# A fixed order for the first job's preparation and the first four attention tiles, and word loads that wait for the first keys

## The chip, the cores and the metric

The program runs on one core of one Trainium2 chip. Its engines work side by side, each from its own queue, in order: TensorE (PE, with its weight loads as PEld), VectorE (DVE), ScalarE (ACT), GpSimd (POOL) and SyncE (SP), which here only issues DMAs. The metric is the device time of one execution in microseconds: 747.5 us for the kernel before, the median of three runs (747.46 to 748.02).

## What is computed

Three layers, one after the other: an attention over 2 batches of 8 heads with 576 rows of 64 columns, in which scores further than tau below their row's maximum are left out; a layer of three products, of which the largest counts, and a fourth product; and four experts, weighted by given shares.

```python
scores = scale * np.matmul(q, k.transpose(0, 1, 3, 2))
thresh = np.max(scores, axis=-1, keepdims=True) - tau
scores = np.where(scores >= thresh, scores, -1000000000.0)
attn = softmax(scores); attn_out = np.matmul(attn, v)
x = attn_out, as 1152 rows of 512
h = np.maximum(np.maximum(x @ w1, x @ w2), x @ w3)
x = h @ w_out
p = domain_probs / (domain_probs.sum(-1, keepdims=True) + 1e-09)
for e in range(4):
    h = np.maximum(x @ m_w1[e], 0.0)
    out += p[:, e:e + 1] * (h @ m_w2[e])
```

`w1`, `w2`, `w3` and `w_out` are 64-bit floats. The kernel loads them as pairs of 32-bit words and makes 32-bit floats of them itself.

## The kernel before

**Stages.** The work on batch 0 comes first. Its attention (stage A, `attention_fast`) has the chip to itself, apart from a little weight preparation. Then come the products on batch 0's rows, with batch 1's attention (`attention_slow`) woven in, and last the products on the rest. All products are matmuls issued at L832.

**Jobs and tiles.** A job is a pair of heads of one batch; stage A has four. A job's 576 rows are 512 main rows and a remainder of 64, and it is worked off in nine tiles: four row chunks for each of the two heads and one tile with both remainders. One tile passes through these steps: scores on PE (`qk`, L301), their negated maximum on DVE (`peak`, L312), the exponential on ACT (`power`, L319), the weighting on DVE, which drops what lies under the threshold and adds up the row (`weigh`, L324), the norm on POOL (`norm`, L332), transposes on PE (`turn`, L342, L345), and the cut of the transposed tile into a high and a low part (`cut_hi`, `cut_lo`; for some tiles through PE, for others through POOL). A group of tiles ends with the product with the values (`gather`, L418). In the code step i does tile i's maximum, the scores of tile i+1 and the cut of tile i-2.

**Preparation of a job.** Queries and keys are split into a high and a low part, transposed on PE and copied out of PSUM to the tiles `K` and `QS` (`prep`; for the first job `prep_first`, L198). Values are split by `values` (L240). The loads are `load_job` and, for the first job, `load_first`, both on SP but for the first queries, which ACT issues. `krem`, `qrem` and `vrem` are the remainders.

**Weight blocks.** A block of the 64-bit weights goes through: its load (`words`, L638), `exponent` on ACT (L646), `clamp` on POOL (L656), the shift `low3` (L653), `merge` (L659) and `sign` (L664) on DVE, `keep`, which writes the 32-bit block back to DRAM (L670), and `hi` and `lo` (L626, L630), which cut it for the matmuls. Each step is put on a list with a due time, counted in columns of products, by a table of lags; the first three blocks have a table of their own (`LAGS_FIRST`). `stream.flush(x)` issues all steps due until x. Up to three blocks (`EARLY`) put their `low3` tile into the PSUM pool of the transposes, and four blocks of words fit at a time (`NW`).

**What sets the order.** In the first attention stage nothing is fixed (`ORDER_A` is empty): the steps are written down in the order of the code, and a scheduler with a clock of its own puts every engine's queue in order. The later stages keep PE, DVE, ACT and POOL in the order of the code. On each engine, SP too, an instruction that waits holds up all that stand behind it. There are eight DMA semaphores, used in turn, so a DMA can't be issued until the eighth one before it has landed.

## Time and profile before

| | |
|---|---|
| Median of three runs | 747.5 us (747.46 to 748.02) |
| The profiled execution | 749.09 us, its span 747.3 us |
| Busy in the span | PE 96%, DVE 51%, ACT 45%, POOL 53% |
| First product matmul | 107.66 us after the start |
| Chain that ended last, share of PE | 77% |

The span is the time from the first to the last instruction of the profiled execution; all times in the rows below count from its start. A row of the timeline gives the start, how long it took, the engine, the line, the operation, the output and inputs, and in brackets how long the engine had been idle and what ended that. `SPq` is SP issuing a DMA, and the time is that of the issue, not of the transfer. In the rows `st_negm` is a tile's maximum, `em` its exponentials, `t` a tile of the transposes' PSUM pool, `a` a cut weight block and `b` the exponent part of one.

### The profile page before, as it was taken

The numbers are of one execution on the slowest core, as the hardware profiler recorded it, in microseconds if no ns is written. First come the engines' busy times: TensorE is split into PE (matmuls) and PEld (weight loads), VectorE is DVE, ScalarE is ACT, GpSimd is POOL, SyncE is SP. The second block draws the span as 40 slices with busy tenths as digits, with TensorE's granted clock in tenths as the row PEclk, the third lists the DMA queues.
The fourth block names the chain that finished last, engine by engine and source line by source line (L and its number), as shares of the span: only waits on it lengthen the run. The fifth ranks groups of instructions, "written<-read, shape, count | busy, mean of one in ns | idle before, by whom it ended". The sixth has DMA issues, their size and how long they took to land.

```text
span 747.3 us, 11716 instructions
## 1 busy us (share of the span) xinstructions
PE 715.7 (96%) x4103; PEld 636.4 (85%) x4103; DVE 378.3 (51%) x900; ACT 339.0 (45%) x716; POOL 392.4 (53%) x435
## 2 busy tenths in 40 slices
PE   4798999999899999999999999999999999999997
PEld 3787889777688788888888899999998998998996
DVE  6798988775265765766766421112222222222222
ACT  5688984444544655465454412333321321321320
POOL 5789785777554555564564524544623522522520
PEclk9799999999999999999999999999999999999999
DMA  6702006876724124122322233223412313312303
GB/s 183 227 22 49 1 1 187 261 226 204 199 78 113 59 73 122 57 73 57 86 61 66 71 113 85 68 58 91 132 50 85 99 43 85 104 45 77 113 2 71
DMA packets 89369, 71.01 MB, mean 95 GB/s; under 512 B 24158, under 2 KB 75358, under 8 KB 89310
## 3 DMA queue, kind: packets, MB, share of 16 engines
q1 hardware_dynamic: 88860, 69.96, 32.7%
q8 instruction: 33, 0.54, 0.3%
q10 hardware_dynamic: 418, 0.30, 0.2%
q14 instruction: 26, 0.21, 0.1%
q0 software_dynamic: 32, 0.00, 0.0%
HBM read 61.59 MB, written 8.65 MB: 94 GB/s over the span
## 4 chain that ended last, share of the span: by engine, by line
PE 77%; DVE 5%; ACT 5%; POOL 5%; issue 3%; DMA 3%; SPq 1%; POOLq 0%; ACTq 0%; DVEq 0%
PE ps L832 63%; PE u L418 5%; PE s L301 4%; PE t L342 3%; POOL a L630 2%; DVE st_negm L312 1%; DMA vrem<-in_v_dram 1%; ACT em L319 1%; DMA words<-in_moe_w_dram 1%; POOL b L656 1%; PE u L175 1%; DMA krem<-in_k_dram 1%; DVE raw L664 1%; ACT a L626 1%; PE t L388 1%
## 5 line engine op out<-in xcount | busy, mean ns | idle before, releaser
L630 POOL TENSOR_TENSOR a<-raw,a 128x512 fp32r<-128x512 f32 (+1 forms) x116 | 145.1, 1256 | 163.6 <-ACT a L626 160.3
L832 PE MATMUL ps<-b,hh 128*128 128x512 f32 x576 | 184.3, 393 | 0.0
L832 PEld LDWEIGHTS ps<-b,hh 128*128 128x128 f32 x576 | 107.3, 188 | 20.4
L782 ACT ACTIVATE hh<-ps 128x320 fp32r<-128x320 f32 (+1 forms) x96 | 46.8, 488 | 152.3 <-PE ps L832 151.9
L832 PE MATMUL ps<-b,hl 128*128 128x512 f32 x288 | 113.1, 393 | 0.0
L832 PE MATMUL ps<-y1h,a 128*128 128x320 f32 x512 | 112.8, 309 | 0.0
L630 POOL TENSOR_TENSOR b<-raw,b 128x512 fp32r<-128x512 f32 x64 | 82.8, 1296 | 53.4 <-ACT b L626 53.4
L785 DVE SCALAR_TENSOR_TENSOR hl<-ps,hh 128x320 fp32r<-128x320 f32 (+1 forms) x96 | 53.4, 556 | 108.9 <-ACT hh L782 108.8
L626 ACT ACTIVATE a<-raw 128x512 fp32r<-128x512 f32 (+1 forms) x116 | 69.4, 612 | 58.8 <-PE ps L832 19.1
L801 DVE SCALAR_TENSOR_TENSOR acc<-ps,pr,acc 128x512 f32<-128x512 f32 x63 | 47.2, 749 | 80.4 <-PE ps L832 80.3
L832 PE MATMUL ps<-y0h,a 128*128 128x512 f32 x256 | 85.1, 403 | 0.8 <-POOL a L630 0.8
L832 PEld LDWEIGHTS ps<-y1h,a 128*128 128x128 f32 x512 | 85.4, 188 | 0.3
L319 ACT ACTIVATE em<-s,st_negm 128x576 f32<-128x576 f32 x72 | 53.3, 744 | 70.9 <-DVE st_negm L312 70.7
L332 POOL TENSOR_SCALAR em<-em,st_r,even 128x576 f32<-128x576 f32 x70 | 57.5, 824 | 43.2 <-DVE st_r L331 41.6
L832 PE MATMUL ps<-y1l,a 128*128 128x320 f32 x256 | 79.1, 309 | 0.0
L312 DVE TENSOR_REDUCE st_negm<-s 128x1 f32<-128x576 f32 x72 | 54.1, 753 | 48.9 <-PE s L301 48.4
L301 PE MATMUL s<-K,QS 128*128 128x288 f32 x320 | 59.7, 315 | 6.4 <-DVE em L324 3.2
L832 PE MATMUL ps<-x1h,a 128*128 128x320 f32 x288 | 63.4, 309 | 0.0
L324 DVE SCALAR_TENSOR_TENSOR em<-s,st_thr,em 128x576 f32<-128x576 f32 x72 | 58.2, 812 | 9.9 <-ACT em L319 7.8
L832 PEld LDWEIGHTS ps<-b,hl 128*128 128x128 f32 x288 | 54.1, 188 | 10.0
L301 PEld LDWEIGHTS s<-K,QS 128*128 128x128 f32 x320 | 49.8, 197 | 11.3 <-issue 6.0
L832 PEld LDWEIGHTS ps<-y0h,a 128*128 128x128 f32 x256 | 47.8, 191 | 9.6 <-POOL a L630 1.2
(129 smaller groups left out, 1271.1 us busy)
## 6 DMA issues: line engine op xcount, KB each, us to landing
raw<-in_moe_w_dram SPq DMA_DIRECT2D x128, 256.0 KB
words<-in_moe_w_dram SPq DMA_DIRECT2D x18, 512.0 KB
kept_w<-raw SPq DMA_DIRECT2D x18, 256.0 KB
raw<-kept_w SPq DMA_DIRECT2D x18, 256.0 KB
kraw<-in_k_dram SPq DMA_DIRECT2D x30, 128.0 KB
words<-in_moe_w_out_dram SPq DMA_DIRECT2D x8, 384.0 KB
vraw<-in_v_dram SPq DMA_DIRECT2D x8, 256.0 KB
qraw<-in_q_dram SPq DMA_DIRECT2D x7, 256.0 KB
```

Source lines behind the costliest of these rows:

```text
L301: nc.tensor.matmul(st.s[:, kh, 0:HS], lhsT=l, rhs=r, start=i == 0, stop=i == len(terms) - 1)
L312: nc.vector.tensor_reduce(out=st.stat["negm"], in_=views(st)[0], op=ALU.max, axis=AX.XY, negate=True)
L319: nc.scalar.activation(out=ev, in_=sv, func=AF.Exp, bias=st.stat["negm"])
L324: nc.vector.scalar_tensor_tensor(out=ev, in0=sv, scalar=st.stat["thr"], in1=ev, op0=ALU.is_ge, op1=ALU.mult, accum_out=st.stat["sum"])
L332: last = (nc.vector if swift else nc.gpsimd).tensor_scalar(out=em, in0=em, scalar1=re, scalar2=even, op0=ALU.mult, op1=ALU.add)
L418: at["valued"] = nc.tensor.matmul(pv, lhsT=l, rhs=r, start=i == 0, stop=i == len(terms) - 1)
L626: nc.scalar.activation(out=b["hi"], in_=b["raw"], func=AF.Copy)
L630: nc.gpsimd.tensor_tensor(out=b["lo"], in0=b["raw"], in1=f32(b["hi"]), op=ALU.subtract)
L782: nc.scalar.activation(out=hs[f][0][:, a:z], in_=ps, func=AF.Relu)
L785: nc.vector.scalar_tensor_tensor(out=hs[f][1][:, a:z], in0=ps, scalar=0.0, in1=f32(hs[f][0][:, a:z]), op0=ALU.max, op1=ALU.subtract)
L801: nc.vector.scalar_tensor_tensor(out=accs[t], in0=ps, scalar=pe, in1=accs[t], op0=ALU.mult, op1=ALU.add)
L832: nc.tensor.matmul(ps, lhsT=l, rhs=r, start=i == 0, stop=i == count - 1)
```

## The change

`prep_first` is written anew: the same operations, in an order that puts the remainder's steps between those of the first head, and cut into pieces by `yield`. From its first piece to the end of the fourth tile's step all five engines, SP among them, keep the order of the code. The first three weight blocks lose their table: each load gets a due time in the head (`FIRST`), and its other steps a due time in one of three turns (`TURN`), which are flushed at set places in the steps of tiles 0, 1, 2 and 3. The constants for tau move behind the first scores, the first job's values into step 1, the second job's loads into the head, and the probabilities' loads behind the third job's. Before its first load of words, a one-column write to the words' tile from `krem` is put on DVE; the load has to wait for it, and it waits for the first keys' remainder.

```diff
-    READY = 20000
+    FIRST, TURN = -60000, -50000
-    LOAD_A, PREP_A, LOAD_B, PREP_B = 0, 1, 1, 3
+    LOAD_A, PREP_0, PREP_A, LOAD_B, PREP_B = 0, 3, 1, 1, 3
...
+        for h in range(2):
+            twin(h)
+            high(h)
+            low(h)
+            tk = turned(ks, h)
+            nc.scalar.activation(out=kd[h], in_=tk, func=AF.Copy)
+            tq = turned(qn, h)
+            if h == 0:
+                twin(2)
+                at["begun"] = kr[:, 1, 0:1]
+                yield
+                high(2)
+                tr = ptile_at("T", [P, 2, P])
+                trk, trq = (tr[:, i, :].rearrange("p (h r) -> p h r", h=2) for i in range(2))
+                nc.tensor.transpose(tr[:, 0, :], flat(kr), ident)
+            nc.scalar.activation(out=qd[h], in_=tq, func=AF.Copy, scale=SCALE)
+            if h:
+                yield
+            nc.vector.tensor_tensor(out=k2[h], in0=tk, in1=f32(kd[h]), op=ALU.subtract)
+            if h == 0:
+                nc.scalar.activation(out=k1r, in_=trk, func=AF.Copy)
+                nc.vector.tensor_tensor(out=k2r, in0=trk, in1=f32(k1r), op=ALU.subtract)
+                yield
+        low(2)
+        nc.tensor.transpose(tr[:, 1, :], flat(QN[:, 2 * NC]), ident)
...
         load_first(jobs[0])
-        stream.flush(-55000)
-        load_job(jobs[0], "v")
+        head = ExitStack()
+        head.enter_context(tc.manual_schedule(engines=set(names.values()) | {ENG.SP}))
         start = prep_first(jobs[0])
         next(start)
+
+        stream.flush(FIRST)
+        next(start)
         qk(steps[0])
+        constants()
+        load_job(jobs[0], "v")
+        stream.flush(FIRST + 1)
+        load_job(jobs[1], "qk")
+        stream.flush(FIRST + 2)
+        load_job(jobs[1], "v")
+        next(start)
+        peak(steps[0])
         for _ in start:
             pass
-        stream.flush(-READY)
-        back.add(values(jobs[0]))
...
+            if 0 < i <= EARLY:
+                stream.flush(TURN + 1000 * i - 1)
             if nxt:
                 power(st)
+            if i < EARLY:
+                stream.flush(TURN + 1000 * i + 100)
             if old:
                 cut_lo(old)
             if nxt:
                 limit(st)
+            if i < EARLY:
+                stream.flush(TURN + 1000 * i + 200)
+            if i == 1:
+                for _ in values(jobs[0]):
+                    pass
...
+            if i == EARLY:
+                head.close()
...
+            if "begun" in at and kept.setdefault("begun", True):
+
+                kept["begun"] = False
+                nc.vector.tensor_scalar(out=b["words"][:, 0, 0, 0:1].bitcast(F32), in0=at["begun"], scalar1=0.0, scalar2=None, op0=ALU.mult)
             nc.sync.dma_start(out=b["words"], in_=src)
...
+        i = kept["planned"] - 1
+        lags = (LAGS64, LAGS_KEPT)[g]
+        if i < EARLY:
+
+            lags = [("words", use - FIRST - i)] + [(nm, use - TURN - 1000 * i - 100 * x) for x, nm in enumerate(("exponent", "clamp", "low3", "merge", "sign", "keep"))] + list(LAGS64[-2:])
```

What this does to three queues follows. The numbers in the names tell buffers apart; line numbers differ between the two kernels (L638 before is L689 now, L129 is L137).

SP, near the start of the program. Before: `words_187` is the third block of words, `words_1839` and `words_1843` the fourth and fifth; `qraw_219`, `kraw_223` and `vraw_231` belong to the second job.

```order
L130 DMA vrem_131<-in_v_dram 128x1x64
L638 DMA words_187<-in_moe_w3_dram 128x4x256
L129 DMA qraw_219<-in_q_dram 128x2x256
L130 DMA qrem_220<-in_q_dram 128x1x64
L129 DMA kraw_223<-in_k_dram 128x4x64 x2
L130 DMA krem_224<-in_k_dram 128x1x64
L129 DMA kraw_223<-in_k_dram 128x4x64 x2
L130 DMA krem_224<-in_k_dram 128x1x64
L670 DMA kept_w0_0_201<-raw_197 128x512
L638 DMA words_1839<-in_moe_w1_dram 128x4x256
L638 DMA words_1843<-in_moe_w2_dram 128x4x256
L129 DMA vraw_231<-in_v_dram 128x2x256
```

And now, from the same DMA on (`words_167` is the second block, `words_181` the third):

```order
L138 DMA vrem_164<-in_v_dram 128x1x64
L689 DMA words_167<-in_moe_w2_dram 128x4x256
L137 DMA qraw_169<-in_q_dram 128x2x256
L138 DMA qrem_170<-in_q_dram 128x1x64
L137 DMA kraw_173<-in_k_dram 128x4x64 x2
L138 DMA krem_174<-in_k_dram 128x1x64
L137 DMA kraw_173<-in_k_dram 128x4x64 x2
L138 DMA krem_174<-in_k_dram 128x1x64
L689 DMA words_181<-in_moe_w3_dram 128x4x256
L689 DMA words_1848<-in_moe_w1_dram 128x4x256
L689 DMA words_1852<-in_moe_w2_dram 128x4x256
L137 DMA vraw_183<-in_v_dram 128x2x256
```

The third block's words moved from ahead of the second job's queries and keys to behind them, and the second job's values now stand behind three blocks of words.

DVE, around the second tile's weighting. Before (`t_209` is the third block's shift, `em_235` the first two tiles' exponentials):

```order
L312 TENSOR_REDUCE st_negm_258<-s_241 128x1
L324 SCALAR_TENSOR_TENSOR em_235,st_sum_238<-s_163,st_thr_237,em_235 128x576
L653 TENSOR_SCALAR t_209<-words_187 128x512
L659 SCALAR_TENSOR_TENSOR t_199<-b_195,t_199 128x512
L315 TENSOR_SCALAR st_thr_259<-st_negm_258,ntau_114 128x1
L330 TENSOR_SCALAR st_sum_238<-st_sum_238 128x1
L664 SCALAR_TENSOR_TENSOR raw_207<-words_128,t_199 128x512
L324 SCALAR_TENSOR_TENSOR em_235,st_sum_260<-s_241,st_thr_259,em_235 128x576
L331 RECIPROCAL st_r_239<-st_sum_238 128x1
```

And now, from the second tile's weighting to the third's (`t_300` is the third block's shift, `t_250` the second's):

```order
L348 SCALAR_TENSOR_TENSOR em_202,st_sum_229<-s_214,st_thr_228,em_202 128x576
L336 TENSOR_REDUCE st_negm_268<-s_235 128x1
L354 TENSOR_SCALAR st_sum_229<-st_sum_229 128x1
L355 RECIPROCAL st_r_230<-st_sum_229 128x1
L710 SCALAR_TENSOR_TENSOR t_250<-b_246,t_250 128x512
L715 SCALAR_TENSOR_TENSOR raw_285<-words_167,t_250 128x512
L339 TENSOR_SCALAR st_thr_269<-st_negm_268,ntau_80 128x1
L704 TENSOR_SCALAR t_300<-words_181 128x512
L348 SCALAR_TENSOR_TENSOR em_267,st_sum_270<-s_235,st_thr_269,em_267 128x576
```

Each tile has one block's merge, sign and the next block's shift between two weightings; the third block's shift moved from ahead of the second tile's weighting to ahead of the third's.

ACT, around the second job's values (`V_569` before, `V_573` now). Before (`em_295` holds the third and fourth tile, `em_373` the fifth, `b_1857` belongs to the fourth block):

```order
L169 ACTIVATE K1_271<-u_290 128x512
L319 ACTIVATE em_295<-s_266,st_negm_296 128x576
L319 ACTIVATE em_295<-s_304,st_negm_336 128x576
L626 ACTIVATE a_1851<-raw_215 128x512
L646 ACTIVATE b_1857<-words_1839 128x512
L246 ACTIVATE V_569<-vraw_231 128x8x64
L252 ACTIVATE VR_570<-vrem_232 64x64 x2
L319 ACTIVATE em_373<-s_344,st_negm_374 128x576
```

And now (`em_267` holds the third and fourth tile, `b_290` belongs to the third block):

```order
L343 ACTIVATE em_267<-s_235,st_negm_268 128x576
L697 ACTIVATE b_290<-words_181 128x512
L673 ACTIVATE a_1856<-raw_285 128x512
L420 ACTIVATE am_282<-t_293 128x4x128
L270 ACTIVATE V_573<-vraw_183 128x8x64
L396 ACTIVATE tcopy_326<-t_303 128x512
L403 ACTIVATE ar_328<-u_308 128x128
L164 ACTIVATE QN_334<-qraw_169 128x4x64 x2
L164 ACTIVATE QN_334<-qrem_170 128x64
L343 ACTIVATE em_267<-s_276,st_negm_311 128x576
```

The values moved from between the fourth and the fifth tile's exponential to between the third's and the fourth's.

## Rows read from the trace of the kernel before

**Rows 1.** The page: busy us of PE and its 40 slices.

```profile
PE 715.7 (96%) x4103; PEld 636.4 (85%) x4103; DVE 378.3 (51%) x900; ACT 339.0 (45%) x716; POOL 392.4 (53%) x435
PE   4798999999899999999999999999999999999997
```

**Rows 2.** Windows: stretch, its length; busy us (instructions) by engine; clock, DMA share, GB/s.

```profile
0.00:10.00 10.00, 3.54 (x15) 2.76 (x16) 3.32 (x12) 3.58 (x8) 2.31 (x11) 1.00 0.68 192
10.00:20.00 10.00, 5.26 (x22) 4.35 (x22) 9.25 (x22) 7.31 (x16) 8.41 (x14) 0.78 0.68 179
20.00:30.00 10.00, 7.12 (x32) 6.25 (x32) 6.83 (x21) 5.71 (x11) 6.51 (x9) 0.54 0.82 257
...
39.00:105.00 66.00, 61.53 (x460) 56.31 (x458) 60.63 (x201) 58.37 (x131) 57.67 (x79) 1.00 0.08 20
...
110.00:120.00 10.00, 10.00 (x79) 10.00 (x80) 7.67 (x16) 4.67 (x12) 1.74 (x2) 1.00 0.24 74
160.00:747.00 587.00, 577.01 (x3239) 514.43 (x3237) 246.31 (x540) 226.29 (x474) 274.11 (x272) 1.00 0.31 87
```

**Rows 3.** Timeline of SP's DMA issues: start, us, line, DMA, count.

```profile
0.74 0.70 SPq L140 DMA_DIRECT2D kraw<-in_k_dram  x1
1.50 0.65 SPq L141 DMA_DIRECT2D krem<-in_k_dram  x1
...
2.81 2.30 SPq L638 DMA_DIRECT2D words<-in_moe_w_dram  x2
...
7.30 1.54 SPq L638 DMA_DIRECT2D words<-in_moe_w_dram  x1
...
11.39 2.39 SPq L129 DMA_DIRECT2D kraw<-in_k_dram  x2
...
16.56 0.54 SPq L130 DMA_DIRECT2D krem<-in_k_dram  x1
...
17.92 1.05 SPq L638 DMA_DIRECT2D words<-in_moe_w_dram  x2
19.06 0.45 SPq L129 DMA_DIRECT2D vraw<-in_v_dram  x1
```

**Rows 4.** Timeline of DVE: first keys, remainder; weightings one, five, six; tenth maximum.

```profile
3.58 0.29 DVE L206 COPY kraw<-kraw 128x256 f32<-128x256 f32 x1 [0.29 <-DMA kraw<-in_k_dram]
...
7.30 0.19 DVE L206 COPY krem<-krem 128x64 f32<-128x64 f32 x1 [2.04 <-DMA krem<-in_k_dram]
...
14.87 0.81 DVE L324 SCALAR_TENSOR_TENSOR em<-s,st_thr,em 128x576 f32<-128x576 f32 x1
...
28.34 0.82 DVE L324 SCALAR_TENSOR_TENSOR em<-s,st_thr,em 128x576 f32<-128x576 f32 x1 [2.35 <-ACT em L319]
...
30.83 0.82 DVE L324 SCALAR_TENSOR_TENSOR em<-s,st_thr,em 128x576 f32<-128x576 f32 x1 [0.43 <-ACT em L319]
...
38.46 0.76 DVE L312 TENSOR_REDUCE st_negm<-s 128x1 f32<-128x576 f32 x1 [0.60 <-PE s L301]
```

**Rows 5.** Timeline of ACT: first exponential, query parts, fourth exponent, second values.

```profile
13.50 0.74 ACT L319 ACTIVATE em<-s,st_negm 128x576 f32<-128x576 f32 x1
...
15.17 0.72 ACT L156 ACTIVATE QN<-qraw 128x256 fp32r<-128x256 f32 x2 [0.17 <-DMA qraw<-in_q_dram]
...
23.71 0.70 ACT L646 ACTIVATE b<-words 128x512 f32<-128x512 f32 x1 [0.31 <-DMA words<-in_moe_w_dram]
25.96 0.63 ACT L246 ACTIVATE V<-vraw 128x512 fp32r<-128x512 f32 x1 [1.55 <-DMA vraw<-in_v_dram]
```

**Rows 6.** Groups of DVE, 10 to 30 us: busy us, mean ns, idle before.

```profile
L653 DVE TENSOR_SCALAR t<-words 128x512 uint32<-128x512 uint32 x3 | 2.1, 688 | 0.3 <-DMA words<-in_moe_w_dram 0.3
L659 DVE SCALAR_TENSOR_TENSOR t<-b,t 128x512 uint32<-128x512 uint32 x3 | 2.1, 684 | 0.0
```

**Rows 7.** Timeline of PE: the first four transposes; the first product matmul.

```profile
3.98 1.09 PE L214 MATMUL u<-ident,kraw 128*128 128x128 f32 x4 [3.98 <-DVE kraw L206]
...
107.66 0.39 PE L832 MATMUL ps<-x0l,a 128*128 128x256 f32 x1
```

More of the change, by code (lines that the diff above doesn't have):

```diff
@@ L46, in fused_kernel @@
     LAGS64 = (("words", 34000), ("exponent", 18500), ("clamp", 16000), ("low3", 14000), ("merge", 13000), ("sign", 11200), ("keep", 11100), ("hi", 10500), ("lo", 9000))
-    LAGS_FIRST = (("words", 60000), ("exponent", 50000), ("low3", 49000), ("clamp", 48000), ("merge", 47000), ("sign", 46000), ("keep", 45000), ("hi", 10500), ("lo", 9000))
     LAGS_KEPT = (("load", 20000), ("hi", 8000), ("lo", 6500))
@@ L91, in fused_kernel, with constants @@
     nc.gpsimd.dma_start(out=tau_c, in_=tau.rearrange("(a o) -> a o", o=1).to_broadcast([P, 1]))
+    neg = cst.tile([P, 1], F32, name="neg")
+    even = cst.tile([P, 1], F32, name="even")
+    ntau = cst.tile([P, 1], F32, name="ntau")
+    def constants():
+        nc.vector.tensor_scalar(out=neg, in0=tau_c, scalar1=0.0, scalar2=None, op0=ALU.is_lt)
+        nc.vector.tensor_scalar(out=even, in0=neg, scalar1=1.0 / S, scalar2=None, op0=ALU.mult)
+        nc.vector.scalar_tensor_tensor(out=ntau, in0=neg, scalar=3e38, in1=tau_c, op0=ALU.mult, op1=ALU.subtract)
     def xy_tiles(g, nm):
@@ L223, in prep_first @@
-        head(0)
-        split(QN[:, 2 * NC:], qr, kr[:, None])
-        tr = ptile_at("T", [P, 2, P])
-        nc.tensor.transpose(tr[:, 0, :], flat(kr), ident)
-        nc.tensor.transpose(tr[:, 1, :], flat(QN[:, 2 * NC]), ident)
-        trk, trq = (tr[:, i, :].rearrange("p (h r) -> p h r", h=2) for i in range(2))
+        qn, qs, ks = ([x(h) for h in range(2)] + [r] for x, r in (
+            (lambda h: QN[:, h * NC:(h + 1) * NC], QN[:, 2 * NC:]), (lambda h: qt[:, h, :, 0, :], qr), (lambda h: kt[:, h], kr[:, None])))
@@ new lines, in twin, with high, low, turned @@
+        def twin(i):
+            nc.vector.tensor_copy(out=ks[i][:, :, 1, :], in_=ks[i][:, :, 0, :])
+        def high(i):
+            nc.scalar.activation(out=qn[i][:, :, 0, :].bitcast(F32R), in_=qs[i], func=AF.Copy)
+        def low(i):
+            nc.vector.tensor_tensor(out=qn[i][:, :, 1, :], in0=qs[i], in1=qn[i][:, :, 0, :], op=ALU.subtract)
+        def turned(x, i):
+            t = ptile_at("U", [P, MAIN])
+            for c in range(NC):
+                nc.tensor.transpose(t[:, c * P:(c + 1) * P], flat(x[i][:, c]), ident)
+            return t
@@ L229, in prep_first @@
+        ko, qo = (0, W + REM), (0, W + 2 * REM)
+        kd, k2, qd = ([t[:, o[h]:o[h] + MAIN] for h in range(2)] for t, o in ((K1, ko), (K2, ko), (QS, qo)))
         k1r, k2r = (t[:, MAIN:MAIN + 4 * REM].rearrange("p (h z) -> p h z", h=2)[:, :, 0:REM] for t in (K1, K2))
         q1r = QS[:, MAIN:MAIN + 6 * REM].rearrange("p (h z) -> p h z", h=2)[:, :, 0:REM]
-        nc.scalar.activation(out=k1r, in_=trk, func=AF.Copy)
-        nc.vector.tensor_tensor(out=k2r, in0=trk, in1=f32(k1r), op=ALU.subtract)
@@ L233, in prep_first @@
-        yield
-        head(1)
+        for h in range(2):
[21 more added lines that the diff above has]
+                yield
@@ L491, in attention_fast @@
             if st and st.j + 1 < len(jobs):
-                if st.r == LOAD_A:
+                if st.r == LOAD_A and st.j:
                     load_job(jobs[st.j + 1])
-                if st.r == PREP_A:
+                    if st.j == 1:
+                        with tc.issue_after(at["loaded"].ins):
+                            load_probs()
+                if st.r == (PREP_A if st.j else PREP_0):
                     front.add(prep(jobs[st.j + 1]))
-            if st:
+            if st and i:
                 peak(st)
```

26 lines of the change are left out of this document (2 added, 24 removed).

## The prediction

> **What bounds the kernel now.** Read the page's first two parts first. TensorE (PE) is busy 96% of the span, and by slices it is short of 9 tenths only in the first few: 4 and 7 tenths in slices 0 and 1, that is before 37 us [rows 1]. Then the windows. PE has 3.54, 5.26 and 7.12 us of work in the first three stretches of 10 us; from 39 to 105 us it has 61.53 of 66.00; from 110 on it is full (10.00 of 10.00, then 577.01 of 587.00) [rows 2]. So after the first attention stage, which ends near 110 us, nothing but PE counts, and what this stage ends earlier or later goes on to the end one to one. Inside the stage no engine alone is the bound: from 39 to 105 us DVE is busy 60.63, ACT 58.37, POOL 57.67 and PE 61.53 of 66 us [rows 2]. A tile passes through all four, in queues that are served in order, so a lag that all of them have can be made up only from their idle time; DVE's is 66.00 − 60.63 = 5.4 us.
>
> The head is different. There DVE works 3.32, 9.25 and 6.83 of each 10 us [rows 2], and single waits decide. The queue's own rows show what SyncE (SP) issues and when [rows 3], the DVE and ACT rows what waited for it [rows 4, 5].
>
> **The gate on the words.** The short key remainder is issued at 1.50 and DVE takes it at 7.30, after 2.04 us of idling for that DMA; two blocks of words, issued from 2.81 on, run beside it [rows 3, 4]. The first keys, with nothing beside them, were issued at 0.74 and taken at 3.58, 2.84 us later [rows 3, 4]. By the same 2.84 us the remainder would be in at 4.3; from 4.3 to 7.3 are the bounds. I take 4.9, since DVE has the keys' copy and the low part of the queries ahead of it. The gate's write follows, and the first words are issued at 5.2 instead of 2.81; behind them on SP stand the first values, the second words and all loads of the next job.
>
> What it removes: the query's low part no longer queues behind the remainder (it could start when ACT's high part is done, about 4.4). With four transposes of 1.09 us [rows 7] for the keys and as many for the queries, two ACT copies and the remainder's short steps, the first tile's scores are complete at about 8.1. Its exponential stands, in the new order, behind the second head's three copies on ACT (each waits for transposes), so it starts at 11.3, where before it started at 13.50 [rows 5]. Its weighting on DVE starts at 12.05 instead of 14.87 [rows 4]. **First term: 2.8 us earlier at the first weighting.**
>
> What hides the later words: a block was read 23.71 − 17.92 = 5.8 us after its issue at the busiest place [rows 3, 5]. From 5.2 that gives 11.0, and DVE comes to it at 10.8: 0.2 us that the exponential covers anyway.
> The Trainium skill ("DMA: Bandwidth & Descriptors", Rules for kernel authors) advises the opposite of this gate: issue a DMA early and wait on its semaphore late. The trace has the first words issued at 2.81 and DVE's shift still idling 0.3 us for them [rows 3, 6]; by the rule the 2.4 us of delay would come through in part (first words 5.2 + 6.8 = 12.0, not 11.0), and the sum below would be +3.1 instead of +2.5.
>
> **One block's steps per tile.** The DVE work of a tile is now maximum 0.75, weighting 0.81, shift 0.69, merge 0.68 [rows 4, 6], sign the same, and about 0.6 of small ones, overlapped by some 0.07 each: 3.9 us. The second weighting is then at 12.05 + 3.9 = 16.0, and the second block's sign ends at 19.1. Nothing is added to DVE but the gate's one-column write; the two orders hold the same DVE instructions ahead of the sixth tile's weighting, so the two times of that weighting can be compared directly. Before, it starts at 30.83 and ends at 31.65 [rows 4].
>
> **The third block's words.** They were issued at 7.30, ahead of the next job's loads [rows 3]; now they stand behind all of its queries and keys. SP is held at the query remainder until DVE has read the old one (its last preparation step, at 10.65 by the walk above). Then come the next job's key loads: four of keys and two of remainders took SP from 11.39 to 16.56 + 0.54 = 17.10, 5.7 us of issuing [rows 3] (the first and the last of four rows). I keep that size: the remainder 0.6, the six 5.7, so the third words are issued at 17.1 and read at 17.1 + 5.8 = 22.9. DVE's shift of this block stands in front of the third tile's weighting and is in order: **DVE idles from 19.1 to 22.9, 3.8 us.** ACT's exponent step of it stands before three more instructions and the next job's values. Bounds of this wait: none, if the six loads were issued at once, to 5 us, if the gate opens only at 7.3.
>
> **The next job's values.** Before, ACT waited 1.55 us for them, reading them at 25.96, 6.9 us after their issue at 19.06; DVE's fifth weighting then had idled 2.35 us [rows 3 to 5]. Now three blocks of words go ahead of them, 0.52 us of issuing each (1.05 for two [rows 3]), so they are issued at 17.1 + 1.6 = 18.7; and the queues hold three blocks of 512 KB where they held two and a kept one of 256 KB, which is 1.0 us more at the 257 GB/s of that stretch [rows 2]. So 18.7 + 6.9 + 1.0 = 26.6. This time the fourth tile's exponential is behind them too: values 0.63, two copies of 0.6 and 0.28 (estimates, from the values' 0.63 for the same 512 columns and about half of it), the query's high parts 0.72 [rows 5] and 0.3 for their remainder, less the overlaps: exponential at 28.8. Behind it come the values' remainder, the fifth exponential (30.0), four more steps of 0.6 to 0.7, among them the copy for which DVE's next instruction waits (33.1), the sixth maximum (33.8) and the sixth exponential (34.6). The sixth weighting ends at about 36.1. **Second term: 36.1 − 31.65 = 4.4 us later there**, the first term already inside. If the values came at once it would be 2 less; if the gate opened at 7.3, 1.2 more.
>
> **What is won back.** At that point ACT has three cuts of 0.6 us more behind it than before. DVE's own work from there to the tenth maximum is 6.3 us, before, that stretch took 38.46 − 31.65 = 6.8 [rows 4]: nothing of weight comes back at once. Over the rest of the stage DVE has the 5.4 us of idle time. Between none and all of 4.4 I take 1.9, the three cuts that ACT is ahead. **Sum: +4.4 − 1.9 = +2.5 us.** Removed waits that are worth nothing by themselves: the loads of the probabilities, moved behind the third job's loads, and the constants, off the path both ways. The planner behind the fourth tile re-sorts the stage; I give that ±1.5 us.
>
> The profiled execution took 749.09 us around its span of 747.3; 749.09 + 2.5 = 751.6 for an execution like it. It lies 1.6 us above the median of the runs, 747.5, so the forecast for the median is 747.5 + 2.5 = **750.0 us**.
>
> **The rivals.**
> *Faster: the waits of DVE and ACT don't come.* Place: the third words and the second values. If the key loads go out faster, and the words are there by 19.1 and the values by about 22, the third weighting starts at 12.05 + 2 · 3.9 = 19.8; DVE has 8.2 us of work from there to the end of the sixth, and 1.5 us go to that tile's scores and exponential: 29.5, 2.2 us before the old one, 745.3. It decides from the moment at which the third words are issued, 13.3 or earlier. For it: 1 MB of words no longer runs beside the first keys, and DVE had 3.2 us idle in 20 to 30 us [rows 2], which a fixed order could fill. Against it: 5.7 us of issuing in the rows.
> *No change: the stage swallows it.* All of the 4.4 us is taken from the 5.4 us of slack: 747.5. For it: the engines are 87 to 93% busy, not full. Against: they wait for each other in a ring.
> *Later still.* The key remainder is late for its own sake, not for the words': the gate opens at 7.3 and delays SP's whole queue, or nothing is won back: 747.5 + 4.4 = 751.9, with both 753.1. For it: nothing but words and queries ran beside the remainder, and it is 32 KB.
>
> **How the numbers follow.** The forecast 0.46, with a range of its own of 748.7 to 751.5; later still 0.13; no change 0.20; faster 0.21. About 0.2%, 1.5 us, is what a measurement of this kernel tells from no change. A little of the forecast's low side falls within it: faster 0.21, same 0.23, slower 0.56. The range, 745.2 to 752.2, reaches down to the faster case and up to the case without recovery.
>
> **What would show it.** Right: the key remainder read near 4.9 and the first words issued near 5.2; the first exponential near 11.3; DVE idle for words at the third shift, around 19 to 23 us; ACT idle for the values around 25 to 26, ahead of the fourth exponential; the sixth weighting near 36; the first product matmul some 2.5 us later than 107.66 [rows 7] and no change in the length of what follows. Wrong: the third words issued by 13 us, a remainder still read at 7, or a stage that ends where it did although the sixth weighting is late.

## The result and the profile after

| | median us | runs, us | ratio to before, 95% interval |
|---|---|---|---|
| before | 747.48 | 4: 745.07 to 748.02 | 1 |
| changed | 755.15 | 4: 753.67 to 756.00 | 1.0107 (1.0080 to 1.0134) |

The change makes the kernel 7.7 us slower. The forecast, 750.0 us, had the sign and a third of the size; its range ended at 752.2. The execution profiled after took 753.67 us around a span of 751.8, 4.6 us more than the one profiled before. The rest of the 7.7 us lies in the choice of executions: the one before was 1.6 us above its median, the one after 1.5 below.

The windows of the changed kernel (columns as in [rows 2]) show where the time is not.

```profile
0.00:10.00 10.00, 5.56 (x21) 4.20 (x21) 3.71 (x13) 4.22 (x8) 2.15 (x10) 1.00 0.44 120
10.00:20.00 10.00, 6.44 (x23) 4.86 (x22) 8.30 (x21) 6.18 (x12) 6.00 (x10) 1.00 0.77 214
20.00:30.00 10.00, 4.21 (x18) 3.89 (x19) 6.44 (x18) 6.41 (x15) 5.87 (x9) 0.63 0.92 302
39.00:105.00 66.00, 59.23 (x444) 54.23 (x442) 58.49 (x193) 55.94 (x128) 54.61 (x78) 1.00 0.11 28
160.00:751.00 591.00, 581.41 (x3259) 518.09 (x3257) 250.72 (x547) 229.10 (x479) 276.48 (x275) 1.00 0.31 88
```

From 160 us on PE is as full as in [rows 2]: the stage behind is unchanged. From 39 to 105 us all engines do less than before (DVE 58.49 instead of 60.63 us): the slack was not used to catch up. The first product matmul says the same in one row; it started at 107.66 [rows 7].

```profile
112.12 0.38 PE L888 MATMUL ps<-x0l,a 128*128 128x256 f32 x1
```

It is 4.46 us later, all that the two spans differ by (4.5). Now the head: SP's issues in the changed kernel (start, duration, line, DMA, count), against [rows 3].

```profile
1.49 0.65 SPq L149 DMA_DIRECT2D krem<-in_k_dram  x1
...
6.66 0.41 SPq L689 DMA_DIRECT2D words<-in_moe_w_dram  x1
...
11.48 1.57 SPq L137 DMA_DIRECT2D kraw<-in_k_dram  x2
...
15.82 0.54 SPq L138 DMA_DIRECT2D krem<-in_k_dram  x1
16.40 1.90 SPq L689 DMA_DIRECT2D words<-in_moe_w_dram  x3
18.40 0.45 SPq L137 DMA_DIRECT2D vraw<-in_v_dram  x1
```

The timeline of DVE, against [rows 4]: the gate's remainder, weightings one and two, the third block's shift, weightings three, four, six, nine, eleven and the last.

```profile
6.25 0.20 DVE L216 COPY krem<-krem 128x64 f32<-128x64 f32 x1 [1.36 <-DMA krem<-in_k_dram]
...
12.34 0.82 DVE L348 SCALAR_TENSOR_TENSOR em<-s,st_thr,em 128x576 f32<-128x576 f32 x1 [0.78 <-ACT em L343]
...
16.04 0.81 DVE L348 SCALAR_TENSOR_TENSOR em<-s,st_thr,em 128x576 f32<-128x576 f32 x1
...
21.56 0.70 DVE L704 TENSOR_SCALAR t<-words 128x512 uint32<-128x512 uint32 x1 [2.34 <-DMA words<-in_moe_w_dram]
22.16 0.81 DVE L348 SCALAR_TENSOR_TENSOR em<-s,st_thr,em 128x576 f32<-128x576 f32 x1
...
27.91 0.82 DVE L348 SCALAR_TENSOR_TENSOR em<-s,st_thr,em 128x576 f32<-128x576 f32 x1 [0.52 <-ACT em L343]
...
33.30 0.82 DVE L348 SCALAR_TENSOR_TENSOR em<-s,st_thr,em 128x576 f32<-128x576 f32 x1 [0.56 <-ACT em L343]
...
40.09 0.82 DVE L348 SCALAR_TENSOR_TENSOR em<-s,st_thr,em 128x576 f32<-128x576 f32 x1 [0.49 <-ACT em L343]
...
49.42 0.81 DVE L348 SCALAR_TENSOR_TENSOR em<-s,st_thr,em 128x576 f32<-128x576 f32 x1
...
111.24 0.82 DVE L348 SCALAR_TENSOR_TENSOR em<-s,st_thr,em 128x576 f32<-128x576 f32 x1
```

And ACT, against [rows 5]: the first exponential, the third block's exponent step, the second job's values, the fourth exponential.

```profile
11.57 0.73 ACT L343 ACTIVATE em<-s,st_negm 128x576 f32<-128x576 f32 x1
...
21.49 0.66 ACT L697 ACTIVATE b<-words 128x512 f32<-128x512 f32 x1 [3.19 <-DMA words<-in_moe_w_dram]
...
25.21 0.63 ACT L270 ACTIVATE V<-vraw 128x512 fp32r<-128x512 f32 x1 [2.06 <-DMA vraw<-in_v_dram]
...
27.14 0.74 ACT L343 ACTIVATE em<-s,st_negm 128x576 f32<-128x576 f32 x1
```

The first weighting is 2.5 us earlier than before. Then come the two waits that the forecast named: for the third words (2.34 us on DVE, 3.19 on ACT) and for the second values (2.06 on ACT). The sixth weighting is 2.47 us late (before: 30.83 [rows 4]), the ninth 0.96, the eleventh 5.30, the last 4.46. In the kernel before, the ninth, the eleventh and the last were:

```profile
39.13 0.81 DVE L324 SCALAR_TENSOR_TENSOR em<-s,st_thr,em 128x576 f32<-128x576 f32 x1
...
44.12 0.81 DVE L324 SCALAR_TENSOR_TENSOR em<-s,st_thr,em 128x576 f32<-128x576 f32 x1
...
106.78 0.82 DVE L324 SCALAR_TENSOR_TENSOR em<-s,st_thr,em 128x576 f32<-128x576 f32 x1
```

The table gives starts of weightings in the profiled executions of the kernels below, and when DVE read the first key remainder, which opens the gate. All are starts from DVE's timeline. One execution of each kernel was profiled; the last column says how far its time lies from the median of its kernel.

| kernel | remainder | 1st | 3rd | 4th | 6th | 11th | last | from the median |
|---|---|---|---|---|---|---|---|---|
| before | 7.30 | 14.87 | 22.70 | 23.73 | 30.83 | 44.12 | 106.78 | +1.6 |
| changed | 6.25 | 12.34 | 22.16 | 27.91 | 33.30 | 49.42 | 111.24 | −1.5 |
| changed, run again | 7.65 | 13.74 | 24.39 | 30.17 | 35.56 | 51.69 | 113.49 | +0.9 |
| preparation early | 6.69 | 12.78 | 23.26 | 30.73 | 36.43 | 47.71 | 111.35 | 0.0 |
| third words early | 6.24 | 12.34 | 19.73 | 30.89 | 35.74 | 51.87 | 113.92 | +2.1 |
| no gate | 6.76 | 12.84 | 22.04 | 27.79 | 33.22 | 49.34 | 111.13 | 0.0 |
| values later | 6.61 | 12.70 | 22.50 | 27.71 | 31.79 | 46.72 | 107.95 | −2.6 |
| third words early, values later | 7.72 | 13.67 | 21.07 | 25.94 | 30.02 | 46.11 | 107.04 | +1.9 |
| the same, preparation at tile 3 | 7.36 | 13.31 | 21.68 | 27.44 | 31.31 | 45.37 | 106.60 | +2.2 |
| POOL relieved | 6.09 | 12.18 | 22.02 | 27.80 | 33.66 | 49.56 | 111.33 | −0.7 |

### The profile page after: what moved, and what is told of

Its sections match the earlier page's. It is cut to its first block, busy times and chain, and to the rows that moved or that the text cites. A ratio compares the mean times of both kernels' runs of the same rounds, so it can differ in the third digit from the quotient of the medians.

```text
span 751.8 us, 11718 instructions
## 1 busy us (share of the span) xinstructions
PE 717.6 (95%) x4103; PEld 637.8 (85%) x4103; DVE 379.2 (50%) x901; ACT 338.5 (45%) x716; POOL 392.5 (52%) x435
## 4 chain that ended last, share of the span: by engine, by line
PE 79%; POOL 6%; DVE 4%; ACT 4%; issue 3%; DMA 2%; SPq 1%; POOLq 0%; ACTq 0%; DVEq 0%
PE ps L888 63%; PE u L442 5%; PE s L325 4%; PE t L366 3%; POOL a L677 2%; DMA vraw<-in_v_dram 1%; ACT em L343 1%; PE u L183 1%; POOL b L707 1%; DVE st_negm L336 1%; ACT a L673 1%; DVE raw L715 1%; POOL em L356 1%; DMA krem<-in_k_dram 1%; PE u L173 1%
```

## The experiments

Kernels of one group ran on one chip, beside runs of the kernel before; ratios are to those.

**First group: 747.39 us before (11 runs).** The second job's preparation begun at the second tile, as in the kernel before:

```
-    LOAD_A, PREP_0, PREP_A, LOAD_B, PREP_B = 0, 3, 1, 1, 3
+    LOAD_A, PREP_0, PREP_A, LOAD_B, PREP_B = 0, 1, 1, 1, 3
```

> The second job's preparation is queued from the second tile on again, as before, and not from the fourth. Everything else is as in the changed kernel. Theory A (the late preparation is what holds up the tenth tile): the tenth weighting, the second job's first, at 44.3 in the changed kernel against 40.8 before, and the eleventh, at 49.4 against 44.1, come 3 us earlier; the kernel lies 3 us or more below the changed one, at 752 or less. Theory B (the waits for the third words and the second values alone carry the loss): the sixth weighting stays near 33.3, nothing is won behind it, and the time stays at 755 within 1 us.

753.76 us, 1.0078 (1.0060 to 1.0095). The eleventh weighting comes 1.7 us earlier, but the sixth 3.1 later and the last where it was: the preparation's work is done ahead of the sixth tile instead of behind it. Beside the changed kernel of this group (755.03 us, below) the intervals overlap: the late preparation by itself does not make the loss.

The third block's words ahead of the second job's queries and keys:

```
-        stream.flush(FIRST + 1)
-        load_job(jobs[1], "qk")
         stream.flush(FIRST + 2)
+        load_job(jobs[1], "qk")
         load_job(jobs[1], "v")
```

> The third block's words are issued ahead of the second job's queries and keys; the planner puts the fourth block's words there too. Theory A: DVE's idle 2.34 us at the third shift goes, the third weighting moves from 22.2 to about 19.8, but the values are still late (25 us or later, since they are behind the same loads) and the preparation of the second job is later still: the tenth weighting moves by less than 1 us and the time stays within 1 us of 755. Theory B: the 2.3 us come through to the end: 752.8 or less.

755.74 us, 1.0104 (1.0081 to 1.0126): nothing won. In the execution profiled, the slowest of four, the third weighting is 2.4 us earlier than in the changed kernel and the fourth 3.0 later. ACT's timeline in this run names the wait that took over:

```profile
25.44 0.63 ACT L270 ACTIVATE V<-vraw 128x512 fp32r<-128x512 f32 x1 [5.20 <-DMA vraw<-in_v_dram]
```

The values are now issued at 21.03 us instead of 18.40, and ACT idles 5.20 us for them ahead of the fourth exponential.

The change without its gate:

```
-            if "begun" in at and kept.setdefault("begun", True):
-                kept["begun"] = False
-                nc.vector.tensor_scalar(out=b["words"][:, 0, 0, 0:1].bitcast(F32), in0=at["begun"], ...)
```

> The one-column write that holds the first load of words until the key remainder is in is left out; every queue keeps its order otherwise. If the gate keeps the words out of the first keys' way: the key remainder is read at 7.2 again and not at 6.25, the first weighting starts at 13.3 instead of 12.34, and the third words, 1.0 to 4 us earlier on SP, land before 20. If the remainder is late for its own sake: it is read at 6.3 as with the gate, and the rest moves up. The time: within 1 us of the changed kernel's 755 if the second job's preparation is the bound, 753 or less if the words are.

753.04 us, 1.0069 (1.0053 to 1.0086). The remainder is read at 6.76, inside the spread that it has with the gate: the words do not delay it.

The changed kernel once more:

> The changed kernel once more, unaltered. Its profiled execution took 753.67 us, 4.6 above that of the kernel before, but the medians lie 7.7 apart. If the executions of one program differ by where a DMA lands in the head, this profile shows the sixth and the tenth weighting 1 to 3 us off those of the first profile (33.30 and 44.26), and the times spread over 3 us again; if not, the weightings are at the same times within 0.3 us and the spread lies elsewhere.

755.03 us, 1.0093 (1.0074 to 1.0113). Its profiled execution took 755.97 us and is a second sample of the same program.

```profile
7.65 0.20 DVE L216 COPY krem<-krem 128x64 f32<-128x64 f32 x1 [2.79 <-DMA krem<-in_k_dram]
...
35.56 0.82 DVE L348 SCALAR_TENSOR_TENSOR em<-s,st_thr,em 128x576 f32<-128x576 f32 x1 [0.56 <-ACT em L343]
...
113.49 0.82 DVE L348 SCALAR_TENSOR_TENSOR em<-s,st_thr,em 128x576 f32<-128x576 f32 x1
```

Its remainder is read 1.40 us later than in the first sample; the sixth weighting is 2.26 later and the last 2.25. In one and the same order, what the head loses goes to the end one to one.

**Second group: 747.12 us before (30 runs).** The second job's values copied behind the sixth exponential (`HELD` = 5), the same for their remainder:

```
+        return tc.issue_after(at["held"].ins) if "held" in at else ExitStack()
...
-        nc.scalar.activation(out=V[:, :, :, 0:D], in_=vn, func=AF.Copy)
+        with behind():
+            nc.scalar.activation(out=V[:, :, :, 0:D], in_=vn, func=AF.Copy)
...
+                        at["held"] = steps[HELD].exp
```

> The changed kernel with one edit: the second job's values are copied on ACT behind the sixth exponential instead of ahead of the fourth, where ACT idled 2.06 us for their load. Nothing is left out. Theory (rigid stage: what the head loses before the sixth weighting goes to the end one to one): the fourth exponential starts about 1.7 us earlier than 27.14, the sixth weighting about 1.7 us earlier than 33.30 for a gate that opens at the same time, and the whole is 1.7 us shorter than the unaltered change, about 753.3 us. Rival (the stage has slack that swallows it): the fourth exponential is earlier, the last weighting is not, 755.0 us as the change. Second rival (the copies of the values only wait in another place): no change at the fourth exponential, because the query copies behind them take the time.

751.66 us, 1.0053 (1.0037 to 1.0070), 3 us less than the change: more than expected. The fourth weighting hardly moves (PE's transposes for the next copy are late there), the sixth is 1.5 earlier and the last 3.3, although the gate opened 0.4 later. This profile is of a fast execution, 2.6 us below the median of twelve.

Both edits, third words early and values later:

> The changed kernel with both waits of its head taken away: the third block's words are issued ahead of the second job's queries and keys, and the second job's values are copied behind the sixth exponential. Nothing is left out. Theory (the two waits in order, third words and then values, make the loss): the third weighting at 19.7 us, the fourth at about 23.3 (before the change: 23.7), the sixth at about 28.5 to 30 (before: 30.8), and 4 to 5 us less than the unaltered change: 750 to 751 us; what is then left over the old 747.4 is the second job's late preparation at the tenth and eleventh weighting and the late opening of the gate. Rival (a further wait stands behind these two: the second job's keys, issued later now, hold the copy on ACT that the sixth maximum waits for): the sixth weighting not before 32 and 753 us or more.

747.79 us, 1.0006 (0.9990 to 1.0021): as fast as the kernel before. DVE, with the remainder as late as 7.72:

```profile
21.07 0.81 DVE L354 SCALAR_TENSOR_TENSOR em<-s,st_thr,em 128x576 f32<-128x576 f32 x1
...
30.02 0.82 DVE L354 SCALAR_TENSOR_TENSOR em<-s,st_thr,em 128x576 f32<-128x576 f32 x1 [0.56 <-ACT em L349]
...
107.04 0.82 DVE L354 SCALAR_TENSOR_TENSOR em<-s,st_thr,em 128x576 f32<-128x576 f32 x1
```

Each against the kernel before in its own group, the four combinations are +7.6 us (neither mended), +8.4 (words), +4.5 (values) and +0.7 (both). The wait for the words stands ahead of that for the values. Mended alone it wins nothing, because the other wait takes its place; the values alone win 3.1 us, both together 6.9. The edit on the values moves their copies too (0.62 and 0.52 us on ACT), not the wait alone.

Both edits, no gate, preparation from the third tile (`PREP_0` = 2):

> As the run with both waits taken away, and besides without the write that holds the words until the first keys are in, and with the second job's preparation begun at the third tile instead of the fourth. Nothing is left out. Theory (four causes that add up: third words, values, gate, late preparation): 2 us less than that run for the gate and 1 to 3 for the preparation: 745 to 748 us, so no slower than the kernel before. Rival (the preparation, begun earlier, waits for keys that are not in yet and stops ACT ahead of the fifth exponential): 750 us or more, with ACT idle for PE at the copy of the keys.

748.29 us, 1.0008 (0.9995 to 1.0022). The last two mendings add nothing.

The gate alone in the kernel before (`at["begun"]` is set behind the copy of the remainder):

```
-        stream.flush(-55000)
-        load_job(jobs[0], "v")
         start = prep_first(jobs[0])
         next(start)
+        stream.flush(-55000)
+        load_job(jobs[0], "v")
...
+                nc.vector.tensor_scalar(out=b["words"][:, 0, 0, 0:1].bitcast(F32), in0=at["begun"], ...)
```

> The kernel before with one part of the change alone: the first words wait, by the same one-column write, until DVE has copied the first key remainder. The order of the engines is otherwise left to the scheduler, which keeps the loads of SyncE in nearly the old order. Nothing is left out. Theory (the gate delays all of SyncE's queue by 4 us and the landing it waits for comes late and unevenly): the first words are read about 3.5 us later than 9.6, the first weighting starts 1.5 to 3 us later than 14.9, and the run is 2 to 3 us slower than the kernel before: 749.5 to 750.5 us. Rival (the gate is free by itself, since the keys come sooner without the words beside them, and only the fixed order behind it makes its delay count): 747.4 us within 0.7.

750.78 us, 1.0044 (1.0028 to 1.0061): the size came out, the way didn't. DVE in this run:

```profile
31.10 0.82 DVE L325 SCALAR_TENSOR_TENSOR em<-s,st_thr,em 128x576 f32<-128x576 f32 x1 [0.49 <-ACT em L320]
...
109.25 0.80 DVE L325 SCALAR_TENSOR_TENSOR em<-s,st_thr,em 128x576 f32<-128x576 f32 x1
```

The sixth weighting is 0.27 us late, the last 2.47. The loss arises behind the head, in an order that the scheduler made anew around the gate. That this order is the cause is argued, not shown.

**Third group: 747.79 us before (29 runs).** Words and values mended, without the gate:

> As the run with third words and values both mended (747.8 us), without the write that holds the first words; the second job's preparation stays at the fourth tile. Nothing is left out. Theory (the gate keeps its price of 2 us, which it had in the unaltered change): 745.8 us. Rival (with the third words ahead of the second job's loads nothing late hangs on the gate any more; what starts the chain is the key remainder, and that is read near 6.8 us with or without the gate): 747.8 us within 0.8.

748.06 us, 1.0006 (0.9996 to 1.0017): the rival. The same with the gate, and preparation from the third tile:

> As the run with third words and values both mended (747.8 us), gate kept, and the second job's preparation begun at the third tile instead of the fourth. Nothing is left out. Theory (the late preparation still costs 2 us at the tenth and eleventh weighting, where that run was 2.0 us behind its own sixth and the kernel before): 746 us. Rival (what the earlier preparation gives at the eleventh weighting the tiles behind lose again, since the engines are over 85% busy there): 747.8 us within 0.8.

746.98 us, 0.9993 (0.9979 to 1.0006): the best version, and no faster than before by what can be measured.

The changed kernel with the remainder loaded first:

```
-            eng.dma_start(out=t[:, 0, :, 0, :], in_=main[:, 0])
             eng.dma_start(out=r[:, 0, :], in_=src[job.b, 2 * job.p:2 * job.p + 2, MAIN:S, :])
+            eng.dma_start(out=t[:, 0, :, 0, :], in_=main[:, 0])
```

> The changed kernel with one edit: the first key and query remainders are loaded ahead of the first halves of keys and queries on both queues, not behind them. Nothing is left out. Theory (the remainder is late because its small packets queue behind the keys on the DMA engines, and the gate opens with it): the remainder is read by 4.5 us instead of 6.25 to 7.65, the first words are issued 2 us earlier, the sixth weighting and the end are 1.5 to 2 us earlier: 753 us. Rival (the remainder's transfer is slow for its own sake, wherever it stands): still read near 6 us, the first keys later by 0.6, and 755 to 756 us.

753.52 us, 1.0076 (1.0059 to 1.0093). Neither as said: now DVE waits for the keys, and reads the remainder behind them at 6.99.

```profile
6.04 0.29 DVE L216 COPY kraw<-kraw 128x256 f32<-128x256 f32 x1 [3.23 <-DMA kraw<-in_k_dram]
```

The same edit in the version with all four mendings:

> As the run with all four causes mended (748.3 us), with the first remainders loaded ahead of the first halves as well. Nothing is left out. Theory (the whole fixed order hangs on the remainder's landing, so an earlier landing moves everything): 746.5 us, less than the kernel before by about 0.6. Rival (other waits of the head decide, such as the transposes of the second half, which ACT waited 1.8 us for): 748.3 us within 0.8.

748.38 us, 1.0012 (0.9998 to 1.0026): no gain.

**Fourth group: 747.02 us before (34 runs).** The change with the first remainders cut by head:

```
-            eng.dma_start(out=r[:, 0, :], in_=src[job.b, 2 * job.p:2 * job.p + 2, MAIN:S, :])
+            for h in range(2):
+                eng.dma_start(out=r[h * REM:(h + 1) * REM, 0, :], in_=src[job.b, 2 * job.p + h, MAIN:S, :])
```

> The changed kernel with one edit: the first key and query remainders, 32 KB each, are loaded in two halves, one DMA for each of the two heads, instead of one DMA whose outermost step is the two heads. Nothing is left out. Theory (the gate opens late because such a DMA runs on 2 of the 16 DMA engines: while it is waited for, the engines' mean busy share is one tenth): the remainder is read at about 4.9 us, which is what the forecast took, instead of 6.25 to 7.65, the first words are issued near 5.2 and the end comes 1.5 to 2.5 us earlier: 753 us. Rival (the remainder is late for another reason, its small packets or the queue's order): still read after 6 us, 755 us.

751.23 us, 1.0058 (1.0040 to 1.0075), 1.8 us below the expected 753, and the mechanism shows. First the DMA engines from 4 to 8 us in the changed kernel (tenths of busy share over all 16, 0.1 us a digit), then in this run, then DVE here:

```profile
DMA  6655799998411111111110000000000000000192
```

```profile
DMA  9998999972000000000000000025459899999999
```

```profile
5.15 0.20 DVE L217 COPY krem<-krem 128x64 f32<-128x64 f32 x1
```

The tail of ones from 5.1 to 6.1 us, in which DVE waits, is gone; the remainder is taken at 5.15 without a wait. The order behind the head differs too, so the gain is not all the gate's.

The same in the best version, in the kernel before, and in the best version without the gate:

> The best version so far (gate kept, third words ahead of the second job's loads, second values copied later, preparation begun at the third tile; 746.98 us), with the first remainders loaded by head. Nothing is left out. Theory (its head hangs on the remainder's landing, read there at 7.36 us): read at 4.9, everything 1.5 to 2.5 us earlier, 745 us, faster than the kernel before by 0.3%. Rival (other waits of the head take its place, such as the second job's queries and keys behind the words on SyncE): 747 us within 0.8.

749.35 us, 1.0028 (1.0017 to 1.0038).

> The kernel before with the first remainders loaded by head, nothing else changed by hand. Nothing is left out. Theory (there too DVE idles 2.04 us for the remainder, but behind it stand two ACT copies and the words): the remainder read near 5 us instead of 7.30 and the end up to 1 us earlier, 746.5 to 747.5 us. Rival (the rest of its head is set by the words and by PE's slow transposes, and the scheduler makes another order from it): 747.6 us within 0.8 or more.

748.44 us, 1.0016 (1.0005 to 1.0027).

> As the mended version with the remainders loaded by head, but without the write that holds the first words. Nothing is left out. Theory (with the remainder landing early the gate costs SyncE's queue 2 us of delay for nothing): 0.5 to 1 us less than the version with the gate, 744.5 us. Rival (the words now run beside the first keys and queries and take back what the halves gave): the same or up to 1 us more, 745 to 746 us.

748.38 us, 1.0021 (1.0009 to 1.0032). In all three the remainder is read early (5.22 to 5.55 us) and the kernel is a little slower than the kernel before, beyond the interval. In the kernel before that is what the rival said; the other two lie above what either side expected. A head that is earlier in a new order is not passed on: in the best version the first weighting moves from 13.31 to 12.25, the last from 106.60 to 107.11.

**Fifth group: 747.35 us before (17 runs).** Why does lateness grow behind the sixth weighting? POOL's first two cuts given to PE and ACT:

```
+    def cycle(names, first=()):
+        yield from first
...
-    for _ in attention_fast(first, cycle(MODES_A)):
+    for _ in attention_fast(first, cycle(MODES_A, ("pe",) * 4)):
```

> The changed kernel with one edit: the first two cuts that POOL makes (a copy of 0.62 and a subtraction of 1.28 us each) are made on PE and ACT instead, as every other cut is. Nothing is left out. Theory (the lateness of the head is not won back but grows by 2 us up to the eleventh weighting because it is POOL that is behind: 14.0 us of work done by 30 us against 17.2 before the change, then no idle time from 31.1 to 41.5 us, and the second job's preparation stands in its queue): POOL reaches that preparation 1.9 us earlier, the sixth weighting stays within 0.5 us for a gate that opens at the same time, the eleventh and the last weighting come 2 to 3.5 us earlier, 752 to 753 us. Rival (DVE and ACT are behind as well and it is they that carry the lateness; the cuts cost ACT 0.6 us each instead): no change, 755 us within 0.8.

753.07 us, 1.0075 (1.0058 to 1.0091), which overlaps the change's interval. POOL's row of the second job's preparation, first in the changed kernel, then here:

```profile
32.87 1.42 POOL L167 TENSOR_TENSOR QN<-qraw,QN 128x256 f32<-128x256 f32 x2
```

```profile
27.87 1.42 POOL L167 TENSOR_TENSOR QN<-qraw,QN 128x256 f32<-128x256 f32 x2
```

It is 5 us earlier, and the eleventh and last weighting do not move (49.56, 111.33). The time is near the one that the theory gave, but not by its way: my theory that POOL carries the lateness falls.

> The best version so far (gate kept, third words early, second values copied later, preparation begun at the third tile; 746.98 us) with POOL relieved of its first two cuts. Nothing is left out. Theory (POOL is what carries the head's lateness there too, 16.2 us of work by 30 us against 17.2): 1 us less, 746 us, which would be below the kernel before. Rival (there POOL is no longer behind and ACT gets 1.2 us more): 747 us within 0.8 or slower.

748.66 us, 1.0012 (0.9996 to 1.0028): no gain there either.

## Why the prediction was wrong

**Right.** The order of events and most of its head: first exponential 11.57 (said 11.3), first weighting 12.34 (12.05), a tile's period 3.7 us (3.9), third words issued at 16.40 (17.1), values read at 25.21 (26.6) with ACT idle 2.06 us ahead of the fourth exponential, PE as full behind the stage as before. Of the sixth weighting's 4.4 us of delay the two samples show 2.47 and 4.73, the second with the gate at 7.65; for a gate at 7.3 the forecast's own terms give 5.6. That the loss hangs on the two waits is shown: with both mended 0.7 us are left, and the interval includes no loss at all.

**Wrong: the gate opens at 4.9.** It opened at 6.25 and 7.65. I gave the remainder the keys' 2.84 us and laid its lateness on the words. In the fixed order it is read at 6.76 to 6.91 without the gate (three runs) and at 6.09 to 7.72 with it (nine): the words held back do not bring it sooner. The rival had this right, though its highest figure, 753.1, falls short too. What the error cost shows where the remainder is cut by head: read at 5.15, the first weighting is at 12.25; read at 6.25, at 12.34; at 7.65, at 13.74. So that the first weighting came out does not bear out the gate's term; in the second sample the error is worth 1.5 us (13.74 less 12.25).

**Wrong, and the step that failed: "What is won back".** I took 1.9 us off, because ACT had three more cuts behind it and DVE 5.4 us of slack. In both samples 2.0 us more are lost from the sixth to the last weighting. Up to the ninth, 1.5 us do come back (2.47 to 0.96; run again, 4.73 to 3.23), where I had said that nothing of weight comes back at once: DVE's work from the sixth weighting to the tenth maximum was 5.66 us in the window 31.65 to 38.46 before, not 6.3. From the ninth to the eleventh, 4.3 us are lost again, in both samples. There stands the second job's preparation, which is queued behind the same two waits and to which I had given no term. I had compared the two orders at the sixth weighting because they hold the same DVE instructions ahead of it. They do; on ACT and PE they do not. ACT's copies of the second job's queries (first head) and keys (second head), before:

```profile
30.69 0.59 ACT L178 ACTIVATE QS<-u 128x512 fp32r<-128x512 f32 x1
...
32.43 0.65 ACT L169 ACTIVATE K<-u 128x512 fp32r<-128x512 f32 x1
```

And in the changed kernel:

```profile
37.63 0.61 ACT L186 ACTIVATE QS<-u 128x512 fp32r<-128x512 f32 x1
...
41.87 0.60 ACT L177 ACTIVATE K<-u 128x512 fp32r<-128x512 f32 x1
```

The sixth weighting is 2.5 us late, these copies 6.9 and 9.4. So a marker like the sixth weighting is not enough: what has not been done by then counts too. Where the preparation begins at the fourth tile, the loss behind the sixth weighting is 1.7 to 2.2 us in all five kernels of the table with the values early; where it begins at the second tile it is −1.0, but the sixth weighting is later by more, and the end is the same. So the place of this loss is shown, not that the late preparation is its cause: with both waits mended it begins at the fourth tile all the same, and costs nothing that can be measured. Which queue carries the lateness behind the marker is open; it is not POOL. DVE's slack did not pay for the lateness.

A rival that no run separates is TensorE's clock. Its granted share in the window 28 to 32 us (1.00 is 2.4 GHz, 0.50 is 1.2 GHz), in the kernel before, the changed one, and the one with both waits mended:

```profile
28.00:32.00 4.00, 3.76 (x25) 3.00 (x24) 3.16 (x11) 2.91 (x7) 2.98 (x5) 0.84 0.85 262
```

```profile
28.00:32.00 4.00, 3.95 (x18) 3.93 (x19) 2.81 (x10) 3.06 (x7) 3.43 (x6) 0.50 0.85 258
```

```profile
28.00:32.00 4.00, 1.95 (x16) 1.75 (x15) 3.40 (x10) 2.57 (x6) 3.92 (x7) 1.00 0.89 301
```

In the changed kernel PE, which had idled up to 3.9 us at a time ahead of this window, works through it at the lower level, and its four score matmuls take 1.31 us (at 29.68) instead of 0.77 (at 34.28). With both waits mended it has the higher level there, and falls once more from 32 to 36 us (0.57). Part of what the two waits cost may go this way. The 1.00 of the changed kernel's first two windows is not borne out by the durations: four transposes take 1.08 us (at 4.00) against 0.60 later (at 36.18).

The forecast also rested on one execution of each kind. Of the 7.7 us, 3.1 are the distance of the two profiled executions from their medians, and a remainder that lands 1.4 us apart is worth 2.25.

The forecast set a rule of the Trainium skill against the gate ("DMA: Bandwidth & Descriptors", Rules for kernel authors): issue a load early, wait for it late. By that rule leaving the gate out should win. In the change it won 2.0 us, with overlapping intervals; with both waits mended it won nothing (1.0006 of the kernel before with the gate and without it).

## What to carry to other kernels

When an order is written out by hand, list for each queue that is served in order what stands behind every load, and mend all such waits of the stretch together: the first of two waits in a row showed no gain by itself. Check at a marker not only when it comes but what each engine still owes there; in a stage whose engines wait for each other, their idle time need not pay for a lateness: here 1.5 us came back and 4.3 went again. And take two profiles of a kernel before a few us are argued from one.

## What the runs showed that was not expected

A 32 KB load, issued 0.75 us behind a 128 KB one, was read 2.6 to 4.2 us behind it. While it is waited for (5.1 to 6.1 us in the changed kernel), the busy share is 0.15 of 16 engines, some two engines (an estimate from that share). Its outermost step is the two heads; cut into one DMA for each head, the tail vanishes and the remainder is there 1.1 to 2.5 us earlier. Placed first, it made the keys behind it late, 6.04 instead of 3.61 us. The Trainium skill states such a rule ("DMA: Bandwidth & Descriptors", Rules for kernel authors): an outermost dimension of fewer than 16 confines the whole DMA to at most that many engines. The trace agrees with it, as far as the mean share of all engines can tell.

Far behind the stage that was changed, TensorE's clock makes executions differ. Near 195 us PE is idle for about half of 5 us. In the changed kernel's profile the granted clock then falls to the lower level (1.2 GHz) for 3.4 us:

```profile
192.00:197.00 5.00, 2.59 (x9) 1.60 (x9) 0.27 (x1) 3.08 (x7) 2.98 (x4) 0.96 0.98 283
197.00:202.00 5.00, 5.00 (x20) 4.02 (x19) 1.71 (x3) 2.90 (x7) 3.96 (x4) 0.70 0.61 179
```

With POOL relieved it doesn't, after nearly the same idle time:

```profile
192.00:197.00 5.00, 2.72 (x11) 1.72 (x10) 0.29 (x1) 3.10 (x7) 3.00 (x4) 1.00 0.96 286
197.00:202.00 5.00, 5.00 (x27) 4.09 (x26) 2.58 (x5) 3.63 (x9) 4.59 (x5) 1.00 0.56 168
```

From the last weighting to the end of the span it is 640.6 us in the first and 639.3 in the second; over all twenty profiles it is 638.7 to 639.4 without such a fall (seven profiles) and 640.1 to 642.2 with one. So two profiles can differ by 1 to 3 us behind the stage that was edited. Why the clock falls in one and not in the other is not shown.
